# Linear attention's phi(k)^T v by two heads at a time, with the high and low halves of both operands side by side

## The chip, the core and the metric

The kernel runs on one core of one Trainium2 chip. The metric is device time in microseconds (us), lower is better. A run's time is that of the whole program. Engines are called by their names in the profile: PE is TensorE (matmul; PEld is its weight load), DVE is VectorE, ACT is ScalarE, POOL is GpSimd, SP is SyncE, whose queue issues most of the loads.

## What is computed

The reference mixes two branches over x (2048 tokens by 1024) with a gate per token. Branch A is linear attention with 32 heads of 32 columns; branch B is a GELU-gated MLP with 3584 hidden columns.

```python
g = _sigmoid((x * gate_w).sum(-1, keepdims=True))
a = _A_ref(x, A_wqkv, A_w_phi, A_wo)
b = _B_ref(x, B_w_gate, B_w_up, B_w_down)
return g * a + (1 - g) * b
```

The change lies in branch A, in the sums over tokens that every query needs:

```python
pk = jnp.einsum("bhsd,hdf->bhsf", k, w_phi)
phi_k = jnp.concatenate([_softmax(pk, axis=-1), _softmax(-pk, axis=-1)], axis=-1)
kv = jnp.einsum("bhsf,bhsd->bhfd", phi_k, v)
z  = jnp.einsum("bhsf->bhf", phi_k)
```

For each head, phi(k) has 64 columns (two softmaxes of 32), v has 32, and kv is a 64 by 32 matrix. z is the sum of phi(k) over the tokens.

## The kernel before

**Split numbers.** Nearly all products are made in the format fp32r. An fp32 operand is split in two fp32r parts: ScalarE copies it to the high part, VectorE subtracts that from the operand and gets the low part (`split`, lines 42 to 44). A product is then three passes: high by high, high by low, low by high (`PASSES`, line 24). Some small products stay in plain fp32: the folds and the sum z.

**Stages.** The first stage makes keys, values, phi(k)^T v and z. The second stage (line 721) makes the MLP's hidden layer and the queries in blocks by a scheme of seven products per 2 by 2 block, with the attention of the queries between them. The third (line 1100) makes the output. In all stages the instructions of PE and DVE run in the order in which the code is written, or put down by a small planner; the other engines' instructions of the first stage are put in order by the framework's scheduler.

**The first stage.** It runs in two halves of 16 heads (`hh`), and in each half over 16 chunks of 128 tokens. Ahead of the chunks, `fold` (lines 184 to 195) multiplies the key weights by w_phi as a block diagonal, so that keys come out as pk. Eight folded weight tiles serve one half. In each chunk:

- `keys_values` (lines 197 to 201): 8 blocks of the contraction by 3 passes by 2 outputs, keys and values, 48 matmuls of 512 columns. Both outputs lie in one PSUM tile of two banks (`two_banks`, line 58), of which there are two.
- `features` (lines 203 to 227), on DVE and ACT: the largest and the smallest pk of each head, the two differences (these four DVE passes read the keys' bank), the exponential (ACT), the split of the values into `vs`, the sums, the reciprocal, the scaling, the split of the features into `f`, and the addition to `zacc`, which collects z per partition.
- `accumulate` (lines 229 to 234): phi(k)^T v for the chunk two before the one whose keys were just made (`pending`). For each group of 4 heads one 128 by 256 block: the stationary operand is 128 columns of the values, the moving one two pieces of 128 features (the two softmaxes). 4 groups by 3 passes, 12 matmuls of 256 columns, into two banks that stay open over the half. Only the diagonal blocks of 32 are used.
- `meanwhile`: one block of x for the next chunks, or one step of the gate (line 171); two gate steps from chunk 11 of the second half on.
- In the second half `query_weights` (lines 275 to 285) folds the query weights, in chunks 3 to 10, with two groups of four plain fp32 products of 128 columns.

The last chunk of the first half is the turn: after each of its 8 contraction blocks comes the fold of one weight tile for the second half, and the features of chunk 14 run in steps between the folds.

**Ends of a half.** `finish_kv` (lines 236 to 240) turns the diagonal 32 by 64 blocks with 16 DVE transposes straight from PSUM into `kv_c`. `finish_z` (lines 242 to 254) multiplies a matrix of ones with `zacc` in plain fp32 and copies the results into `zb` by eight small ACT copies. Behind the second half (lines 374 to 390) TensorE makes the first projections of the MLP with what is left of the attention between them: g0, phi(k)^T v of chunk 14, g1, u0, z, phi(k)^T v of chunk 15, u1. POOL stores `kv_c` and `zb` to DRAM (lines 388 and 389), where the second stage reads them.

**The joint.** The second stage's buffers take the place of the first stage's. Lines 609 to 614 load four blocks of x (`raw`), the fourth into memory that the first stage's last tiles held; lines 466 to 469 are the sums of these blocks, lines 399 and 402 the high and low parts of sums and weights.

**Queues.** SP issues loads in program order; one that waits for memory holds up all behind it. POOL issues stores.

**PSUM.** Eight banks: two tiles of two banks (tag `pd`) for keys and values, four single banks (tag `pg`) of which phi(k)^T v holds two and folds, z and projections use the others.

Of the kernel before, what the change touches and what calls it, by code (L numbers as in the profile page):

```python
# [31 lines left out]
def tile_gated_mix(ctx: ExitStack, tc: tile.TileContext, x, xT, wkT, wqT, wv, w_phi, wo,  # L32
# [22 lines left out]
    def bank():  # L55
        return psum_g.tile([P, BLK], F32, tag="pg", name="pg", bufs=4)

    def two_banks():
        return psum_d.tile([P, 2, BLK], F32, tag="pd", name="pd", bufs=2)
# [77 lines left out]
    def fold_query(s, bp, k, pf):  # L137

        for j in range(4):
            nc.tensor.matmul(pf[:, j * P:(j + 1) * P], s[:, (4 * k + j) * P:(4 * k + j + 1) * P],  # L140
                             bp.rearrange("p a b -> p (a b)"), start=True, stop=True)
        nc.scalar.activation(s[:, k * BLK:(k + 1) * BLK], pf, AF.Copy)
# [3 lines left out]
    with tc.tile_pool(name="kw", bufs=1) as kw, tc.tile_pool(name="kp", bufs=1) as kp, \  # L146
            tc.manual_schedule(engines={PE, DVE}):
        ones = kp.tile([P, P], F32, name="ones")
        nc.vector.memset(ones, 1.0)
        phi_c = kp.tile([P, NG, 32], F32, name="phi_c")  # L150

        warm = two_banks()
        for _ in range(7):
            nc.tensor.matmul(warm[:, 0, :P], ones, ones, start=True, stop=True)
# [11 lines left out]
        kv_c = kp.tile([P, NG, 2, 32], F32, name="kv_c")  # L166
# [17 lines left out]
        def fold(hh, kc, bd, s=None):  # L184
# [3 lines left out]
            pf = bank()  # L188
# [8 lines left out]
        def keys_values(ps, w, b, t, kc):  # L197
            for i, (a, e) in enumerate(PASSES):
                for m in range(2):
                    nc.tensor.matmul(ps[:, m, :], xb[b, kc // 4][:, a, kc % 4, t * P:(t + 1) * P], w[:, e, m * 512:(m + 1) * 512],  # L200
                                     start=kc == 0 and i == 0, stop=kc == KC - 1 and i == 2)

        def features(ps, vs, f, zacc, first):

            pk = ps[:, 0, :].rearrange("p (h f) -> p h f", f=32)
# [8 lines left out]
            split(vs[:, 0, :], vs[:, 1, :], ps[:, 1, :])  # L214
# [14 lines left out]
        def accumulate(pkv, vs, f, first, last):  # L229
            for j in range(4):  # L230
                for i, (a, q) in enumerate(PASSES):
                    nc.tensor.matmul(pkv[j // 2][:, j % 2], vs[:, a, j * P:(j + 1) * P], f[:, q, :, j * P:(j + 1) * P],  # L232
                                     start=first and i == 0 and j % 2 == 0, stop=last and i == 2,
                                     skip_group_check=True)

        def finish_kv(hh, pkv):
            for j in range(4):
                for h in range(4):
                    q = slice(32 * h, 32 * h + 32)
                    nc.vector.transpose(kv_c[q, 4 * hh + j], pkv[j // 2][q, j % 2, :, 32 * h:32 * h + 32])  # L240

        def finish_z(hh, zacc):
            if hh:
                pz = two_banks()
                pz = [pz[:, s, :] for s in range(2)]
            else:
                pz = [bank() for s in range(2)]
            for s in range(2):
                nc.tensor.matmul(pz[s], ones, zacc[:, s].rearrange("p h f -> p (h f)"), start=True, stop=True)
            for s in range(2):  # L250
                z4 = pz[s].rearrange("p (g h f) -> p g h f", g=4, h=4)
# [23 lines left out]
        def query_weights(n):  # L275
            if staged:
                g, s, bp = staged.pop()
                for k in range(2):
                    fold_query(s, bp, k, bank())
                nc.gpsimd.dma_start(wq_fold[g], s)  # L280
            if 1 < n < 2 + NG:
                g = n - 2
# [6 lines left out]
        for hh in range(2):  # L289
            chunks = [(b, t) for b in ((0, 1, 2, 3) if hh == 0 else (2, 3, 0, 1)) for t in range(4)]  # L290
            ahead = []
            if hh == 0:

                ahead = [two_banks(), two_banks()]
# [28 lines left out]
            for n, (b, t) in enumerate(chunks):  # L323
# [3 lines left out]
                else:  # L327
                    ps = two_banks()
# [813 lines left out]
```

## Time and profile before

| | |
|---|---|
| median of 3 runs | 2396.36 us (2395.64 to 2396.86) |
| span of the execution profiled, the own time used below | 2395.1 us |
| PE busy | 2387.5 us, 10817 matmul records |
| first stage's key and value matmuls (line 200) | 1536 of 512 columns, from 8.6 to 429.0 us |
| phi(k)^T v (line 232) | 384 of 256 columns, from 47.9 to 451.5 us |
| DVE busy between 420 and 460 us | 37.7 of 40 us |
| first product of the second stage (line 721) | at 478.82 us |

The profile is one execution. A timeline row gives the start in us from the span's start, the length, the engine, the line of the kernel, the operation, the tile written and the tiles read, the shapes and the count; in brackets stand the idle time of the engine ahead of it and what ended it. A row of grouped instructions gives, behind the count, the busy time in us and the mean in ns of one instruction, then the idle time in front. A row of waits reads: who waited, for what, us in total, times, the longest. Matmuls overlap in their records, so the cost of one is read from the distance between starts. Plain fp32 matmuls appear as two records each.

### The profile page before, as it was taken

Reading aid. Unit: us, or ns where it says so; the run is one execution under the profiler, and the core shown is the slowest. Engines: PE = TensorE matmul, PEld = TensorE weight load, DVE = VectorE, ACT = ScalarE, POOL = GpSimd, SP = SyncE. Lnnn points to the kernel's source line nnn. Section 1 sums busy time; section 2 is a strip of 40 time slices with the busy share of each in tenths; the row PEclk is TensorE's granted clock in tenths of the full one; section 3 lists DMA queues with packets and bytes.
Section 4 is the critical chain, followed back from the end, with each engine's and each line's share of the span. In section 5 each row is a group of like instructions: output and inputs, shape, how many; then the busy total and the mean of one; then the engine's idle time right before and its main releaser. Section 6 shows DMA issues by size and latency. Waiting matters only on the chain.

```text
span 2395.1 us, 28363 instructions
## 1 busy us (share of the span) xinstructions
PE 2387.5 (100%) x10817; PEld 1986.0 (83%) x10817; DVE 1748.3 (73%) x2203; ACT 985.0 (41%) x1276; POOL 157.4 (7%) x294
## 2 busy tenths in 40 slices
PE   9999999999999999999999999999999999999999
PEld 8888888888888888888888888888888888888887
DVE  6877767857877877778777777777674778867873
ACT  4323232345454544455555555555533223323221
POOL 0000000011111112100000000000000000000000
PEclk9999999999999999999999999999999999999999
DMA  4112232544445456564334443443685767977874
GB/s 170 53 45 88 71 121 84 179 172 159 169 153 179 165 201 221 204 237 166 129 133 142 147 146 133 143 146 129 234 297 185 256 218 254 332 275 280 277 270 138
DMA packets 152569, 425.11 MB, mean 177 GB/s; under 512 B 21360, under 2 KB 21360, under 8 KB 152432
## 3 DMA queue, kind: packets, MB, share of 16 engines
q1 hardware_dynamic: 123840, 329.30, 40.7%
q0 software_dynamic: 27552, 93.87, 10.2%
q8 instruction: 84, 1.38, 0.2%
q14 instruction: 53, 0.43, 0.1%
q10 hardware_dynamic: 1040, 0.13, 0.0%
HBM read 328.34 MB, written 94.90 MB: 177 GB/s over the span
## 4 chain that ended last, share of the span: by engine, by line
PE 94%; DVE 3%; DMA 1%; ACT 1%; issue 1%; SPq 0%; ACTq 0%; DVEq 0%
PE po L1100 29%; PE a L721 20%; PE pd L200 14%; PE c L721 13%; PE b L721 7%; PE p L721 7%; PE misc L883 2%; PE pg L232 2%; PE pg L190 1%; PE pg L140 1%; DMA stage<-in_w_up 0%; DMA raw<-in_xT 0%; DMA stage<-in_w_gate 0%; DVE stage L171 0%; DMA early<-in_wkT 0%
## 5 line engine op out<-in xcount | busy, mean ns | idle before, releaser
L200 PE MATMUL pd<-wkv,x 128*128 128x512 f32 x1536 | 359.6, 392 | 0.0
L200 PEld LDWEIGHTS pd<-wkv,x 128*128 128x128 f32 x1536 | 286.3, 189 | 58.3 <-issue 0.5
L1100 PE MATMUL po<-tw,wgu 128*128 128x512 f32 x1344 | 309.8, 389 | 0.0
L1100 PEld LDWEIGHTS po<-tw,wgu 128*128 128x128 f32 x1344 | 252.3, 188 | 52.4
L399 ACT ACTIVATE wgu<-stage 128x1024 fp32r<-128x1024 f32 x147 | 155.1, 1055 | 244.7 <-DVE stage L990 160.4
L402 DVE TENSOR_TENSOR wgu<-stage,wgu 128x1024 fp32r<-128x1024 f32 x147 | 179.5, 1221 | 79.6 <-ACT wgu L399 78.6
L402 DVE TENSOR_TENSOR tyz<-stage,tyz 128x1024 fp32r<-128x1024 f32 x126 | 153.0, 1214 | 41.8 <-ACT tyz L399 41.8
L399 ACT ACTIVATE tyz<-stage 128x1024 fp32r<-128x1024 f32 x126 | 132.7, 1053 | 117.1 <-DVE stage L547 64.5
L721 PE MATMUL a<-s,tyz 128*128 128x512 f32 x744 | 179.4, 390 | 0.8 <-DVE tyz L402 0.4
L721 PE MATMUL b<-s,tyz 128*128 128x512 f32 x744 | 178.9, 389 | 0.1
L721 PE MATMUL a<-x,wgu 128*128 128x512 f32 x744 | 178.8, 389 | 0.0
L721 PE MATMUL c<-x,tyz 128*128 128x512 f32 x744 | 178.7, 389 | 0.0
L721 PE MATMUL p<-s,tyz 128*128 128x512 f32 x744 | 178.7, 389 | 0.0
L721 PE MATMUL a<-s,v 128*128 128x512 f32 x744 | 178.7, 389 | 0.0
L721 PE MATMUL c<-x,wgu 128*128 128x512 f32 x744 | 178.7, 389 | 0.0
L721 PEld LDWEIGHTS a<-s,tyz 128*128 128x128 f32 x744 | 139.4, 188 | 30.8 <-DVE tyz L402 1.3
L721 PEld LDWEIGHTS b<-s,tyz 128*128 128x128 f32 x744 | 139.6, 188 | 29.5 <-ACT b L756 0.5
L721 PEld LDWEIGHTS a<-x,wgu 128*128 128x128 f32 x744 | 139.6, 188 | 29.2 <-DVE h L696 0.2
L721 PEld LDWEIGHTS p<-s,tyz 128*128 128x128 f32 x744 | 139.7, 188 | 29.0
L721 PEld LDWEIGHTS c<-x,tyz 128*128 128x128 f32 x744 | 139.6, 188 | 29.0
L721 PEld LDWEIGHTS c<-x,wgu 128*128 128x128 f32 x744 | 139.6, 188 | 29.0
L721 PEld LDWEIGHTS a<-s,v 128*128 128x128 f32 x744 | 139.6, 188 | 29.0
(170 smaller groups left out, 3461.1 us busy)
## 6 DMA issues: line engine op xcount, KB each, us to landing
stage<-lm SPq DMA_DIRECT2D x98, 512.0 KB, 4.6
sr<-in_w_down SPq DMA_DIRECT2D x84, 512.0 KB, 5.0
sl<-lm SPq DMA_DIRECT2D x70, 512.0 KB, 4.8
lm<-h POOLq DMA_DIRECT2D x112, 256.0 KB, 2.5
stage<-in_w_gate SPq DMA_DIRECT2D x43, 512.0 KB, 3.7
stage<-in_w_up SPq DMA_DIRECT2D x43, 512.0 KB, 4.1
stage<-la SPq DMA_DIRECT2D x28, 512.0 KB, 4.8
tg<-stage POOLq DMA_DIRECT2D x26, 512.0 KB, 3.0
```

The costliest lines, as they stand in the source:

```text
L140: nc.tensor.matmul(pf[:, j * P:(j + 1) * P], s[:, (4 * k + j) * P:(4 * k + j + 1) * P], bp.rearrange("p a b -> p (a b)"), start=True, stop ...
L190: nc.tensor.matmul(pf[:, j * P:(j + 1) * P], s[:, j * P:(j + 1) * P], bd[:, j].rearrange("p a b -> p (a b)"), start=True, stop=True)
L200: nc.tensor.matmul(ps[:, m, :], xb[b, kc // 4][:, a, kc % 4, t * P:(t + 1) * P], w[:, e, m * 512:(m + 1) * 512], start=kc == 0 and i == 0, ...
L232: nc.tensor.matmul(pkv[j // 2][:, j % 2], vs[:, a, j * P:(j + 1) * P], f[:, q, :, j * P:(j + 1) * P], start=first and i == 0 and j % 2 == ...
L399: nc.scalar.activation(dst, src, AF.Copy)
L402: nc.vector.tensor_tensor(dst, src, dst_h.bitcast(F32), OP.subtract)
L721: nc.tensor.matmul(dst, w[:, h, 4 * part + kc, :], xq[:, e, kc, :], start=first and kc == 0 and i == 0, stop=kc == 3 and i == 2, skip_grou ...
L883: nc.tensor.matmul(po, kbs[:, a, s, :], pts[:, q, s, :], start=s == 0 and i == 0, stop=s == 1 and i == 2)
L1100: nc.tensor.matmul(ps[c], lefts[s][:, a, m, c * P:(c + 1) * P], made[k][:, e, m], start=d == 0 and m == 0 and n == 0, stop=d == n_duo - 1 ...
```

## The change

Five things are changed, all in the first stage.

1. phi(k)^T v: `vs` holds, for each pair of heads, 64 high columns and 64 low columns of the values side by side, which make one stationary operand of 128 columns. The moving operand is the high and low parts of both softmaxes' features of the same two heads, four pieces of 64 columns. One matmul per pair of heads makes all four combinations of parts, low by low too: 8 matmuls of 256 columns per chunk. The results lie in four open banks, which take the whole tag `pg`.
2. `finish_kv` adds the halves: ACT copies the columns of the high features, DVE adds those of the low features, ACT copies the rows of the low values beside those of the high ones, DVE adds them, then two wider transposes. The store is made by `finish_kv` itself, for each half, by two DMAs.
3. Keys and values lie in single banks (tag `pd`, now four of one bank). Outside the turn and the start, all 24 key matmuls come ahead of the 24 value matmuls. The folds of the turn, the query folds (one behind the keys, one behind the values, from chunk 4 on), the first z and the first projections use these four banks as well.
4. z: `zacc` is split into two parts in a weight buffer of the second stage or in one of `f`, and multiplied with ones in fp32r, two passes. At the end the order is g0, phi(k)^T v of chunk 14, the split of z, g1, u0, phi(k)^T v of chunk 15, u1, z.
5. ACT's copy of a folded query weight is marked urgent for the scheduler.

The core of the diff:

```diff
         def keys_values(ps, w, b, t, kc, parts=range(2)):
             for i, (a, e) in enumerate(PASSES):
-                for m in range(2):
-                    nc.tensor.matmul(ps[:, m, :], xb[b, kc // 4][:, a, kc % 4, t * P:(t + 1) * P], w[:, e, m * 512:(m + 1) * 512],
+                for m in parts:
+                    nc.tensor.matmul(ps[m], xb[b, kc // 4][:, a, kc % 4, t * P:(t + 1) * P], w[:, e, m * 512:(m + 1) * 512],
...
-            split(vs[:, 0, :], vs[:, 1, :], ps[:, 1, :])
+            split(vs[:, :, 0], vs[:, :, 1], ps[1].rearrange("p (a b) -> p a b", b=64))
...
         def accumulate(pkv, vs, f, first, last):
-            for j in range(4):
-                for i, (a, q) in enumerate(PASSES):
-                    nc.tensor.matmul(pkv[j // 2][:, j % 2], vs[:, a, j * P:(j + 1) * P], f[:, q, :, j * P:(j + 1) * P],
-                                     start=first and i == 0 and j % 2 == 0, stop=last and i == 2,
-                                     skip_group_check=True)
+            for d in range(8):
+                heads = slice(64 * d, 64 * d + 64)
+                nc.tensor.matmul(pkv[d // 2][:, d % 2], vs[:, d].rearrange("p a b -> p (a b)"), f[:, :, :, heads],
+                                 start=first and d % 2 == 0, stop=last, skip_group_check=True)
 
         def finish_kv(hh, pkv):
-            for j in range(4):
-                for h in range(4):
-                    q = slice(32 * h, 32 * h + 32)
-                    nc.vector.transpose(kv_c[q, 4 * hh + j], pkv[j // 2][q, j % 2, :, 32 * h:32 * h + 32])
+            t = kp.tile([P, 4, 2, 2, 64], F32, tag="e", name="kv_t", bufs=2)
+            for n, p in enumerate(pkv):
+                nc.scalar.activation(t[:, n], p[:, :, 0], AF.Copy)
+                nc.vector.tensor_tensor(t[:, n], p[:, :, 1], t[:, n], OP.add)
+            low_rows = kp.tile([P, 4, 2, 2, 64], F32, tag="e", name="kv_l", bufs=2)
+            nc.scalar.activation(low_rows[:64], t[64:], AF.Copy)
+            nc.vector.tensor_tensor(t[:64], t[:64], low_rows[:64], OP.add)
+            kv_c = kp.tile([P, 4, 2, 2, 32], F32, name="kv_c")
+            for h in range(2):
+                q = slice(32 * h, 32 * h + 32)
+                nc.vector.transpose(kv_c[q].rearrange("p a b c d -> p (a b c) d"),
+                                    t[q].rearrange("p a b c d -> p (a b c) d")[:, :, q])
+            for d in range(2):
+                nc.gpsimd.dma_start(kz[0][64 * d:64 * d + 64, 4 * hh:4 * hh + 4], kv_c[:64, :, d])
...
+        def z_parts(zacc, zs):
+            zs = zs.rearrange("p i (s a) b -> p i s (a b)", s=2)
+            split(zs[:, 0], zs[:, 1], zacc.rearrange("p s h f -> p s (h f)"))
+            return zs
+        def finish_z(hh, zs, parts=range(2)):
+            for s in parts:
+                pz = bank() if hh else turn_bank()
+                for i in range(2):
+                    nc.tensor.matmul(pz, ones_r, zs[:, i, s], start=i == 0, stop=i == 1)
...
-                    for kc in range(KC):
-                        keys_values(ps, wkv[kc], b, t, kc)
-                        if turn:
-                            fresh.append(fold(1, kc, bd))
+                        for kc in range(KC):
+                            keys_values(ps, wkv[kc], b, t, kc)
+                            fresh.append(fold(1, kc, bd, pf=turn_bank()))
                             next(steps, None)
+                    else:
+                        for m in range(2):
+                            for kc in range(KC):
+                                keys_values(ps, wkv[kc], b, t, kc, (m,))
+                            if hh:
+                                query_weights(n, m)
+                            if hh and n == 1:
+                                finish_z(0, zs, (m,))
...
-                        finish_z(0, zacc)
+                        zs = z_parts(zacc, new_weight())
...
-        first_g = {0: project(first_w[0], 0)}
+        first_g = {0: project(first_w[0], 0, turn_bank())}
         pending.pop(0)()
-        first_g[1] = project(first_w[0], 1)
-        pu = two_banks()
-        first_u = {0: project(first_w[1], 0, pu[:, 0, :])}
+        zs = z_parts(zacc, kp.tile([P, 2, KC, P], F32R, tag="f", name="zs", bufs=2))
+        first_g[1] = project(first_w[0], 1, turn_bank())
+        first_u = {0: project(first_w[1], 0, turn_bank())}
...
         second_w = weight(w_gate[1])
-        finish_z(1, zacc)
         pending.pop(0)()
-        nc.gpsimd.dma_start(kz[0], kv_c)
+        first_u[1] = project(first_w[1], 1, turn_bank())
+        finish_z(1, zs)
         nc.gpsimd.dma_start(kz[1], zb)
-        first_u[1] = project(first_w[1], 1, pu[:, 1, :])
```

More of the change, by code (lines that the diff above doesn't have):

```diff
@@ L165, in tile_gated_mix @@
         spare = [kp.tile([P, 1024], F32, tag="gw", name="early", bufs=1)] + spare
-        kv_c = kp.tile([P, NG, 2, 32], F32, name="kv_c")
         zb = kp.tile([P, NG, 2, 32], F32, name="zb")
@@ L273, in tile_gated_mix, with query_weights @@
         staged = []
-        def query_weights(n):
+        def query_weights(n, k):
             if staged:
[L277 to L282, printed above, removed]
+                g, s, bp = staged[0]
+                fold_query(s, bp, k, turn_bank())
+                if k:
+                    nc.gpsimd.dma_start(wq_fold[g], s)
+                    staged.pop()
+            if k and 2 < n < 3 + NG:
+                g = n - 3
                 bp = kp.tile([P, 4, 32], F32, name="bp", bufs=2)
@@ L292, in tile_gated_mix @@
             if hh == 0:
-                ahead = [two_banks(), two_banks()]
+                ahead = [[turn_bank(), turn_bank()] for _ in range(2)]
                 early = {}
@@ L366, in values @@
                     if n == 0:
-                        pkv += [psum_g.tile([P, 2, 2, P], F32, tag="pg", name="pg", bufs=4) for _ in range(2)]
+                        pkv += [bank((P, 2, 2, 2, 64)) for _ in range(4)]
                     accumulate(pkv, vs, f, n == 0, n == 15)
```

42 lines of the change are left out of this document (17 added, 25 removed).

## The prediction, made before the changed kernel ran

> **What bounds the kernel now.** I read the head of the page first, then the chain of work that ended last, then what TensorE waited for, then the timelines of the first stage.
>
> ```profile
> span 2395.1 us, 28363 instructions
> PE 2387.5 (100%) x10817; PEld 1986.0 (83%) x10817; DVE 1748.3 (73%) x2203; ACT 985.0 (41%) x1276; POOL 157.4 (7%) x294
> PE 94%; DVE 3%; DMA 1%; ACT 1%; issue 1%; SPq 0%; ACTq 0%; DVEq 0%
> ```
>
> TensorE is never free: 94% of the chain is its own work. So time comes off by taking matmuls away, as long as nothing else is late when TensorE comes earlier. The change touches only the first stage (keys, values and phi(k)^T v, up to about 460 us). What TensorE waits for at the joint behind that stage:
>
> ```profile
> PE a L721 <- DVE tyz L402: 0.4, 1, 0.4
> PE a L721 <- ACT c L754: 0.3, 1, 0.3
> ```
>
> Short, but not harmless: a wait of 0.4 us on VectorE says that VectorE's work there is just in time, with no slack to give.
>
> One chunk of 128 tokens, the turn between the halves (line 190 folds the second half's weights), and the sums z, on TensorE's timeline (start, length, form):
>
> ```profile
> 185.10 11.07 PE L200 MATMUL pd<-wkv,x 128*128 128x512 f32 x48
> 196.01 1.59 PE L232 MATMUL pg<-f,vs 128*128 128x256 f32 x12
> 197.44 1.55 PE L200 MATMUL pd<-wkv,x 128*128 128x512 f32 x6
> ...
> 229.37 1.88 PE L249 MATMUL pg<-zacc,ones 128*128 128x512 f32 x4
> 230.68 11.48 PE L200 MATMUL pd<-wkv,x 128*128 128x512 f32 x48
> 242.00 1.60 PE L232 MATMUL pg<-f,vs 128*128 128x256 f32 x12
> ```
> ```profile
> 448.45 1.88 PE L249 MATMUL pd<-zacc,ones 128*128 128x512 f32 x4
> 449.77 1.99 PE L232 MATMUL pg<-f,vs 128*128 128x256 f32 x12
> 451.59 5.63 PE L107 MATMUL pd<-x,wgu 128*128 128x512 f32 x24
> 457.06 21.92 PE L107 MATMUL pg<-x,wgu 128*128 128x512 f32 x96
> ```
>
> Starts are to be subtracted, since lengths overlap. 48 key and value matmuls: 196.01 - 185.10 = 10.91 us, 0.227 each. The 12 of phi(k)^T v: 197.44 - 196.01 = 1.43 us, 0.119 each.
>
> **The product phi(k)^T v.** Before, four groups by three passes make 12 matmuls of 256 moving columns per chunk. After, eight pairs of heads make 8, again of 256 columns: high and low values fill the stationary side, high and low features the moving side. Four fewer by 0.119 us, in 32 chunks: 4 x 0.119 x 32 = 15.2 us, all on the path. The Trainium skill ("TensorE: Matmul & The Clock Gate", section Back-to-back issue gap) gives a warm gap of N / 2.4 + 2.5 ns, 109 ns for 256 columns; by that estimate the sum would be 14.0 us. The trace's 0.119 differs from it and is used.
>
> **z.** The pair of fp32 products costs TensorE 230.68 - 229.37 = 1.31 us, and the group behind it starts slowly: 242.00 - 230.68 = 11.32 against 10.91. Together 1.72; at the end 1.32 and 1.82 - 1.43, 1.71. After, four split matmuls of 512 columns: 4 x 0.227 = 0.91. Saved twice: 1.6 us. TensorE's work shrinks by 15.2 + 1.6 = 16.8 us.
>
> **Keys, then values.** The same 48 matmuls, in runs into one bank. Line 107 runs 96 into single banks from 457.06; its group of 24 ahead takes 457.06 - 451.59 = 5.47, 0.228 each, so nothing here, within 0.9 us either way (0.03 per chunk). What it moves is VectorE: the four passes over the keys can start while the values are still being multiplied.
>
> ```profile
> 380.05 0.69 DVE L207 TENSOR_REDUCE mm<-pd 128x16 f32<-128x512 f32 x1 [2.26 <-PE pd L200]
> 384.21 0.69 DVE L44 TENSOR_TENSOR vs<-pd,vs 128x512 fp32r<-128x512 f32 x1 [0.53 <-ACT vs L43]
> 392.39 0.69 DVE L207 TENSOR_REDUCE mm<-pd 128x16 f32<-128x512 f32 x1
> 431.92 0.69 DVE L207 TENSOR_REDUCE mm<-pd 128x16 f32<-128x512 f32 x1
> ...
> 435.46 0.69 DVE L466 TENSOR_TENSOR raw<-raw 128x512 f32<-128x512 f32 x1
> ...
> 452.53 0.68 DVE L466 TENSOR_TENSOR raw<-raw 128x512 f32<-128x512 f32 x1
> 453.13 4.15 DVE L240 STREAM_TRANSPOSE kv_c<-pg 32x64 f32<-32x64 f32 x16
> 457.31 0.69 DVE L467 TENSOR_TENSOR raw<-raw 128x512 f32<-128x512 f32 x1
> 468.14 0.69 DVE L466 TENSOR_TENSOR raw<-raw 128x512 f32<-128x512 f32 x1 [2.82 <-DMA raw<-in_xT]
> ```
>
> In chunk 11 of the second half VectorE waits for TensorE until 380.05 and reads the values at 384.21, 4.2 us after they were ready. After, it reads them as soon as ScalarE has copied them:
>
> ```profile
> L43 ACT ACTIVATE vs<-pd 128x512 fp32r<-128x512 f32 x32 | 18.7, 584 | 0.0
> L44 DVE TENSOR_TENSOR f<-e,f 128x1024 fp32r<-128x1024 f32 x32 | 39.2, 1226 | 37.4 <-ACT f L43 37.4
> L43 ACT ACTIVATE f<-e 128x1024 fp32r<-128x1024 f32 x32 | 33.9, 1058 | 79.7 <-DVE e L220 79.6
> L254 ACT ACTIVATE zb<-pd 32x128 f32<-32x128 f32 x8 | 2.2, 270 | 2.7 <-PE pd L249 2.6
> L210 DVE TENSOR_TENSOR e<-pd,mm 128x512 f32<-128x512 f32 x32 | 21.8, 681 | 0.0
> L284 DVE TENSOR_TENSOR bp<-phi_c,mask 128x128 f32<-128x128 f32 x8 | 2.3, 284 | 0.0
> ```
>
> That is 0.7 us after their end (0.58 for the copy and a hand-over): 3.5 us won against TensorE. From chunk 11 on the chunks carry two gate steps, and VectorE's own period (392.39 - 380.05 = 12.34, with 0.1 idle) is longer than TensorE's new one (12.34 - 0.48 = 11.9). So from there VectorE runs back to back, and TensorE only fixes its starting point.
>
> **The joint.** The last step of the chunks is the turn of phi(k)^T v into its stored form, and its store frees the memory that the next stage loads into. The sync queue shows it (waits, then its issues):
>
> ```profile
> SPq L461 <- DMA kz<-zb: 19.3, 1, 19.3
> SPq L461 <- DMA kz<-kv_c: 4.6, 1, 4.6
> ```
> ```profile
> 435.57 0.34 SPq L51 DMA_DIRECT2D stage<-in_w_up  x1
> 460.00 0.88 SPq L461 DMA_DIRECT2D raw<-in_xT  x2
> 460.93 1.45 SPq L51 DMA_DIRECT2D stage<-in_w_gate  x2
> ```
> ```profile
> 457.58 0.55 POOL L388 DMA_DIRECT2D kz<-kv_c  x1 [4.13 <-DVE kv_c L240]
> ```
>
> The queue stands from 435.9 to 460.0, last for kv_c's store, with two weight loads behind the waiting one. The block of x lands at 468.14, and VectorE is then busy up to the product that waited 0.4 us. So this chain sets TensorE's next stage, and I follow its shift:
> - Chunk 11 ends earlier by 25 accumulations (16, then 9) x 0.476 + 0.8 for the first z = 12.7 us. VectorE wins 3.5 more: its last chunk (431.92) starts 16.2 us earlier.
> - Behind it the low part of z is new on VectorE (one pass of 1024: 1.2, ScalarE's 1.06 ahead of it filled by sums of x, as such waits are now).
> - Instead of 16 transposes (457.31 - 453.13 = 4.2) stand four adds of 256 (0.35 each, between the rows of 512 and 128; 1.4), a wait for ScalarE's copy of the low rows (1.06), an add of 1024 (1.2) and two transposes of 512 (0.7 each: 4.15 / 16 = 0.26 for 64 columns, and 448 more at the 1.03 ns that 681 - 284 over 384 columns gives; 1.4): 5.0, so 0.8 more. Behind the wait for ScalarE stand the sums of x; nobody but this store waits for its end. Two stores instead of one: 0.55 more on POOL.
> - Sum 1.2 + 0.8 + 0.55 = 2.6, so the load leaves 16.2 - 2.6 = 13.6 us earlier, at 446.4. z's own store, now behind the last accumulation and one projection, needs: the last accumulation's end, 451.59 - 15.2 - 0.8 - 1.7 = 433.9, the projection's 5.5, z's 0.9, ScalarE's eight copies at 2.2, and 2.7 to the store's end (457.31 to 460.0 for kv_c): 445.2, just ahead of it.
>
> TensorE would be 16.8 earlier, the chain 13.6: 3.2 us of TensorE's gain are waited away at the joint. Bounds: 4.4 if ScalarE's 1.06 ahead of the low part isn't filled, 0 if the sums of x that now precede 453.13 are put behind the store. I take 3.2, by the rows.
>
> **Banks.** phi(k)^T v holds all four banks of one pool, so folds go through the four single banks with keys and values. At the turn two dedicated banks become the two of chunk 14, whose values are read behind the first fold's parts:
>
> ```profile
> 201.01 0.68 DVE L44 TENSOR_TENSOR wkv<-pg,wkv 128x512 fp32r<-128x512 f32 x1
> 201.61 0.68 DVE L44 TENSOR_TENSOR vs<-pd,vs 128x512 fp32r<-128x512 f32 x1
> ```
> ```profile
> 201.10 1.05 PE L190 MATMUL pg<-bd,stage 128*128 128x128 f32 x8
> ...
> 203.37 1.05 PE L190 MATMUL pg<-bd,stage 128*128 128x128 f32 x8
> ```
>
> Folds are due every 203.37 - 201.10 = 2.3 us. Chunk 14's keys are read ahead of the turn, so the first fold has its bank; the second needs that of chunk 14's values, read last of the three VectorE passes behind the first fold (1.9 us with ScalarE's copy among them, and 1.4 us of matmuls to cover it): 0.5 (0 to 1.1). In the query chunks the keys' bank is back after VectorE's first 2.4 us (four passes of 0.6) and a fold's after one ScalarE copy, while at least 24 x 0.227 = 5.4 us of matmuls pass between two uses: nothing, and what a late bank would cost is rival 2. ScalarE's strided writes of the values and the copy marked urgent cost nothing, covered by ScalarE's idle time (41% busy); a copy slower by 0.1 us would, uncovered, cost 0.5 over the last five chunks, where VectorE waits for it. The copy of ones to fp32r at the start is one pass of 128 columns (0.28 at most) while TensorE runs its warm-up on the plain ones: nothing.
>
> Sum: 16.8 - 3.2 - 0.5 = 13.1 us, so 2395.1 - 13.1 = 2382.0 for the execution profiled. It stands 1.3 us under the median of 2396.36, which gives 2383.3.
>
> **Rivals.**
> 1. The joint moves with TensorE. If the scheduler puts the store of kv_c ahead of the sums of x, or z's store alone gates the load, all 16.8 us come out, with 0.9 for longer runs perhaps: 2396.4 - 16.8 - 0.9 = 2378.7 at best, 2379.5 as the value. For it: from 435.46 to 452.53 VectorE does eleven pieces of the next stage ahead of the store. Against: none of its rows from 431.92 to 457.31 has idle time in front, so it has no room to reorder into.
> 2. Banks in strict turn. At chunk 1 of the second half VectorE does the new turn of kv (5.0 us) ahead of the four key passes (2.4), and only then gives the bank back. If chunk 2's keys are handed that bank, TensorE stands 7.9 us: 2391.2. Against it: the z banks are free much earlier.
> 3. Slower: the moving operand. f is now read in four pieces of 64 columns, where it was two of 128. If TensorE pays for pieces, line 232's 256 remaining matmuls carry it. From 0.119 to 0.189 each the forecast gain and 4.8 us more are gone (17.9 / 256 = 0.070); at twice the pitch, 0.238, it is 30.5 more, 2413.8. Against it: two pieces already run at 0.119, near half of the 0.227 of 512 unbroken columns. The Trainium skill ("Advanced Engine Details and Errata", Memory Cachelines) says that a non-contiguous access pattern significantly slows matmuls, in its part on PSUM; the two-piece rows show nothing of it on the SBUF side.
> That the change leaves the work undone can't be: the four passes fewer are in the loop's count.
>
> **How the numbers follow.** A measurement here can tell about 0.2%, 4.8 us, from no change. Forecast 0.60, rival 1 0.18, rival 2 0.10, rival 3 0.05, unnamed stalls 0.07. Rival 2 lies at the edge, half faster and half the same; of the stalls 0.03 faster, 0.03 same, 0.01 slower. Faster 0.60 + 0.18 + 0.05 + 0.03 = 0.86, same 0.08, slower 0.06. The range goes from rival 1's best, 2378.5, to just past rival 2, 2392, and leaves out rival 3 and most stalls.
>
> **What would show it.** Line 232's successor: 256 matmuls, groups of 8 in 0.95 us. TensorE idle some 3 us at the joint, waiting on VectorE or ScalarE, with the last x load issued near 446. VectorE's key passes starting before the values end. Wrong: waits of keys_values for VectorE in the loop, a pitch above 0.13, or a joint with no new wait.

## The result and the profile after

| | before | after |
|---|---|---|
| median of 4 runs each | 2396.0 us (2395.05 to 2396.86) | 2383.35 us (2382.01 to 2385.03) |
| span of the execution profiled | 2395.1 | 2381.9 |

After takes 0.9949 of before's time, 95% interval 0.9935 to 0.9963: 12.65 us less by the medians, 13.2 by the two profiled spans. Forecast were 2383.3 and 13.1.

The head of the page after the change, to hold against that of before:

```profile
span 2381.9 us, 28130 instructions
PE 2370.9 (100%) x10689; PEld 1969.3 (83%) x10689; DVE 1748.3 (73%) x2188; ACT 994.1 (42%) x1288; POOL 158.8 (7%) x297
```

TensorE is busy for 16.6 us less (2387.5 - 2370.9); VectorE has as much to do as before. Less than 16.6 came out, so TensorE stands somewhere. What it waits for at the joint, from 425 to 500 us (total, times, longest):

```profile
PE c L698 <- DVE h L647: 2.3, 1, 2.3
PE a L739 <- DVE wgu L420: 0.6, 1, 0.6
PE a L739 <- ACT c L772: 0.4, 1, 0.4
```

That is 3.3 us, where before has only the 0.3 for ScalarE there: a new wait of 3.0. (The 0.4 us on VectorE's `tyz` that the prediction read as the joint's lies later in the second stage in both kernels, at 678.64 in before and 664.60 in after.) Later on, after has 0.7 us of waits in the third stage that are in neither before nor a second profile of the same kernel (e11, below): they belong to that execution.

TensorE's timeline after (start, length; starts are to be subtracted): the turn of the halves, the second half's first chunks with the products of z (line 264), and the end of the first stage.

```profile
188.85 1.11 PE L235 MATMUL pg<-f,vs 128*128 128x256 f32 x8
189.81 1.55 PE L202 MATMUL pd<-wkv,x 128*128 128x512 f32 x6
...
208.42 1.20 PE L235 MATMUL pg<-f,vs 128*128 128x256 f32 x8
...
226.79 0.62 PE L264 MATMUL pd<-wgu,ones_r 128*128 128x512 f32 x2
227.24 5.60 PE L202 MATMUL pd<-wkv,x 128*128 128x512 f32 x24
...
431.85 1.12 PE L235 MATMUL pg<-f,vs 128*128 128x256 f32 x8
432.81 5.63 PE L107 MATMUL pd<-x,wgu 128*128 128x512 f32 x24
438.27 1.07 PE L264 MATMUL pg<-zs,ones_r 128*128 128x512 f32 x4
439.18 22.20 PE L107 MATMUL pg<-x,wgu 128*128 128x512 f32 x96
```

Eight products take 0.96 us, 0.120 each (before: 0.119); z takes 0.45 twice in the first half and 0.91 at the end; the turn takes 208.42 - 189.81 = 18.61, where before it took 215.51 - 197.44 = 18.07 by the same rows. The list of TensorE's waits has no line for keys and values (202), so no chunk of the second half waits for a bank.

VectorE at the end of the first stage, in the order of time:

```profile
414.63 0.69 DVE L209 TENSOR_REDUCE mm<-pd 128x16 f32<-128x512 f32 x1
...
421.86 0.69 DVE L484 TENSOR_TENSOR raw<-raw 128x512 f32<-128x512 f32 x1 [1.87 <-DMA raw<-in_xT]
...
430.35 1.22 DVE L44 TENSOR_TENSOR zs<-zacc,zs 128x1024 fp32r<-128x1024 f32 x1
...
436.39 1.41 DVE L243 TENSOR_TENSOR kv_t<-pg,kv_t 128x256 f32<-128x256 f32 x4
...
439.04 1.21 DVE L246 TENSOR_TENSOR kv_t<-kv_t,kv_l 64x1024 f32<-64x1024 f32 x1
...
440.78 1.41 DVE L250 STREAM_TRANSPOSE kv_c<-kv_t 32x512 f32<-32x512 f32 x2
...
454.11 0.69 DVE L484 TENSOR_TENSOR raw<-raw 128x512 f32<-128x512 f32 x1 [2.91 <-DMA raw<-in_xT]
```

and the stores (POOL) and the load that stands for them (SP):

```profile
442.48 1.27 POOL L253 DMA_DIRECT2D kz<-kv_c  x2 [74.72 <-DVE kv_c L250]
443.74 0.56 POOL L408 DMA_DIRECT2D kz<-zb  x1
```
```profile
446.29 0.88 SPq L479 DMA_DIRECT2D raw<-in_xT  x2
```
```profile
467.26 0.50 PE L698 MATMUL c<-x 128*128 128x512 f32 x1 [2.32 <-DVE h L647]
```

The load leaves at 446.29; the forecast was 446.4. But the tail has grown. Call the **lag** the time from the end of the last accumulation (the start of what follows it on TensorE) to this load. Before it was 460.0 - 451.59 = 8.4 us, after it is 446.29 - 432.81 = 13.5: VectorE begins the turn 3.6 behind the accumulation (1.5 before), takes 5.8 to its end at 442.2 (4.2 before), and three stores leave behind one another.

The product of line 698, where TensorE waits, hangs on this load: in all twelve profiles that wait there it starts 20.75 to 21.04 us behind the load's issue (467.26 - 446.29 = 20.97 in after). In before it started 21.54 behind it and waited for nothing (481.54 - 460.00), so the chain there had an estimated 0.6 us of slack (21.54 less some 20.9).

**A start that differs.** The two profiles also differ where both kernels do the same. Stretches of the first microseconds of before; behind the busy times and counts of five engines stand the granted TensorE clock, the DMA share and GB/s:

```profile
7.00:8.00 1.00, 0.82 (x5) 0.82 (x6) 1.00 (x2) 0.22 (x1) 0.00 (x0) 0.73 0.93 318
8.00:9.00 1.00, 1.00 (x6) 1.00 (x6) 0.75 (x2) 0.41 (x1) 0.00 (x0) 0.50 1.03 389
9.00:10.00 1.00, 1.00 (x4) 0.81 (x3) 0.43 (x2) 0.93 (x2) 0.00 (x0) 0.50 1.06 412
10.00:11.00 1.00, 1.00 (x4) 0.75 (x4) 1.00 (x3) 0.71 (x2) 0.00 (x0) 0.56 1.05 406
11.00:12.00 1.00, 1.00 (x11) 0.95 (x9) 0.60 (x1) 0.00 (x0) 0.00 (x0) 1.00 1.05 397
```

and of after:

```profile
8.00:12.00 4.00, 4.00 (x26) 3.32 (x24) 3.55 (x6) 3.47 (x6) 0.00 (x0) 1.00 1.05 404
```

In before's profile the clock was at half for 0.54 + 1 + 1 + 0.88 = 3.4 us (0.54 and 0.88 being twice what 0.73 and 0.56 lack to one); in after's it wasn't. Of the 13 profiles of this study, before, e6 and e8 have the dip; the other ten, among them two of the same changed kernel, don't. It also shows in executions of one kernel: of the 39 executions of before that ran beside the experiments, 36 list a mean granted clock of 1.000 and have a median span of 2393.6, three list 0.999 (3.4 us at half in 2395 make 0.9993) and have 2394.4, 2394.5 and 2396.1. In e1, though, three executions with 0.999 are no longer than the other two. So the dip belongs to the execution and not to the kernel, and its price is less sure than its length. The Trainium skill ("TensorE: Matmul & The Clock Gate", Part 1) states a free-running window of 3.4 us whose position varies from run to run; the length agrees with these rows. In the profiles that have it, everything behind it is later: the accumulation that starts at 188.85 in after starts at 190.37 in e6, whose code up to there is the same; the last one ends 1.1 to 1.3 later (434.07 against 433.02 and 432.81), and 1.3 later in e8 than in e9 (433.70 against 432.37). So an estimated 1.2 us of the 13.2 between the two profiled spans, and of every shift read between them, are this and not the change.

### The profile page after: what moved, and what is told of

It is laid out like the page before. It is cut to its first block, busy times and chain, and to the rows that moved or that the text cites. A ratio compares the mean times of both kernels' runs of the same rounds, so it can differ in the third digit from the quotient of the medians.

```text
span 2381.9 us, 28130 instructions
## 1 busy us (share of the span) xinstructions
PE 2370.9 (100%) x10689; PEld 1969.3 (83%) x10689; DVE 1748.3 (73%) x2188; ACT 994.1 (42%) x1288; POOL 158.8 (7%) x297
## 4 chain that ended last, share of the span: by engine, by line
PE 75%; issue 3%; DMA 1%; DVE 1%; POOL 0%; ACT 0%; SPq 0%; POOLq 0%; DVEq 0%; ACTq 0%
PE po L1118 27%; PE a L739 20%; PE c L739 13%; PE b L739 7%; PE p L739 7%; PE misc L901 2%; DMA sr<-in_w_down 1%; POOL lm L135 0%; DVE sr L1040 0%; DVE tyz L420 0%; DMA lm<-h 0%; ACT tyz L417 0%; POOL la L135 0%; ACT L867 0%; DVE x L883 0%
```

## The experiments

Times are medians; "last acc." is the end of the last accumulation, "load" the issue of the x load, "joint" what TensorE waits from 425 to 500 us; "dip" marks the profiles with half the clock at the start (all in us, from the profile).

| run | time | ratio to before (95%) | last acc. | load | lag | joint |
|---|---|---|---|---|---|---|
| before (dip) | 2396.00 | | 451.59 | 460.00 | 8.4 | 0.3 |
| after | 2383.35 | 0.9949 (0.9935 to 0.9963) | 432.81 | 446.29 | 13.5 | 3.3 |
| e11, after again | 2382.69 | 0.9948 (0.9936 to 0.9961) | 433.02 | 446.43 | 13.4 | 3.2 |
| e1 | 2382.75 | 0.9946 (0.9934 to 0.9959) | 432.80 | 446.00 | 13.2 | 3.3 |
| e2 | 2380.87 | 0.9939 (0.9926 to 0.9951) | 432.88 | 444.29 | 11.4 | 1.5 |
| e3 | 2391.45 | 0.9984 (0.9975 to 0.9994) | 432.61 | 454.37 | 21.8 | 9.4 |
| e4 | 2399.33 | 1.0015 (1.0006 to 1.0024) | 448.19 | 462.23 | 14.0 | 3.6 |
| e5 | 2384.79 | 0.9956 (0.9943 to 0.9968) | 434.67 | 446.82 | 12.2 | 2.7 |
| e6 (dip) | 2383.86 | 0.9953 (0.9941 to 0.9966) | 434.07 | 448.96 | 14.9 | 3.8 |
| e7 | 2382.43 | 0.9947 (0.9933 to 0.9960) | 435.50 | 446.30 | 10.8 | 1.7 |
| e8 (dip) | 2380.61 | 0.9942 (0.9929 to 0.9954) | 433.70 | 445.46 | 11.8 | 1.8 |
| e9 | 2380.22 | 0.9936 (0.9923 to 0.9950) | 432.37 | 443.53 | 11.2 | 1.3 |
| e10 | 2379.25 | 0.9936 (0.9923 to 0.9948) | 432.33 | 442.94 | 10.6 | 0.8 |

Beside e1 to e4, run on one chip, before took 2395.41; beside e5 to e8 2395.43; beside e9 to e11 2395.10.

**e1: the block of x in other memory.** If the load stands because its buffer takes the place of z's or kv's, another place sets it free.

```diff
+        raw4 = fp.tile([P, 2, 2 * BLK], F32, tag="pts", name="raw", bufs=1)
         xs = [(xa if k < 2 else fp).tile(...) for k in range(4)]
...
-        raws.append(fp.tile([P, 2, 2 * BLK], F32, tag="pts", name="raw", bufs=1))
+        raws.append(raw4)
```

> Only the place of the fourth block of x is changed: its buffer is put ahead of two others, so that it falls on memory of the folded weights, which is free after the last key and value matmul. Theory (the joint is held by the stores of kv_c and z, which hold the sync queue): the queue no longer stands from 419 to 446 us, the block lands before 430, TensorE's waits at the joint (3.3 us in sum) fall to under 1 us, and the time falls by 2.5 us (1.5 to 3.3), to 2380.9. Rival (VectorE's amount of work at the joint is the bound, the load only fills a hole): the waits stay near 3 us and the time at 2383.3. Rival (time follows TensorE's work alone): 2383.3.

It left at 446.00, with the same waits behind it, and its queue still stood 25.9 us for kv_c's store and 0.9 for z's. The edit so did not set the load free, and the theory about the stores is not tested by it. Either a load into this pool waits for the last stores wherever in the pool it lies, or the new place overlaps what they read as well; no trace shows the addresses, and another pool wasn't tried.

**e2: the gate's passes behind the turn of kv.** In after, VectorE does two gate passes and sixteen small copies from 432 to 435, in front of the turn. The edit moves them behind the stores.

```diff
-        nc.scalar.activation(g_a, logit, AF.Sigmoid)
-        (g_b, g_n and the 16 copies to g_at)
         second_w = weight(w_gate[1])
         ...
         nc.gpsimd.dma_start(kz[1], zb)
+        nc.scalar.activation(g_a, logit, AF.Sigmoid)
+        (g_b, g_n and the 16 copies to g_at)
```

> The eighteen small VectorE passes of the gate (3.1 us) go from ahead of the turn of kv to behind it. Theory: kv_c's store leaves up to 3.1 us earlier; z's store, bound by TensorE's order (products until 439.2, copies until 441.7), then gates the load at about 444.3 instead of 446.3: 2.0 us less (1.0 to 2.5), 2381.3. Rival (VectorE's amount of work is the bound): the same work in another order, 2383.3.

VectorE's rows:

```profile
434.52 1.41 DVE L243 TENSOR_TENSOR kv_t<-pg,kv_t 128x256 f32<-128x256 f32 x4
...
438.80 1.41 DVE L250 STREAM_TRANSPOSE kv_c<-kv_t 32x512 f32<-32x512 f32 x2
...
440.40 3.25 DVE L408 COPY g_at<-g_a 32x16 f32<-32x16 f32 x16
```

The load leaves at 444.29, 2.0 us earlier, though TensorE's last accumulation ended at the same place (432.88). The waits at the joint shrink from 3.3 to 1.5, and the time from 2383.35 (2382.69 in e11) to 2380.87. So what VectorE does ahead of the turn sets when the load leaves, and the 2.0 us come back nearly one for one. (Of the 3.1 us that were moved the turn gained 1.9, 434.52 against 436.39: two more sums of x now stand ahead of it.)

**e3: the opposite dose.** The sixteen copies done twice, at their old place.

```diff
                 nc.vector.tensor_copy(g_at[...], g_a[...])
+                nc.vector.tensor_copy(g_at[...], g_a[...])
```

> The sixteen small copies of the gate are done twice: 3.0 us more on VectorE ahead of the turn of kv. Theory (VectorE up to kv_c's store sets the joint, with no slack): the store and the load behind it leave 2.9 us later, TensorE waits 6 us at the joint instead of 3.3, the time rises by 2.9 us (2.3 to 3.2) to 2386.2. Rival (time follows TensorE's work): VectorE has idle time at 446 and 451 us that takes it up, 2383.3.

The dose came out larger than meant: sums of x were scheduled between the copies, and the turn began at 444.53 instead of 436.39, 8.1 us later. The load left at 454.37, 8.1 later, and the time is 2391.45, 8.1 over after's 2383.35. TensorE stands in a second place too, since z's products need a bank that the adds give back:

```profile
445.10 2.05 PE L264 MATMUL pg<-zs,ones_r 128*128 128x512 f32 x4 [6.86 <-DVE kv_t L243]
...
475.37 0.50 PE L699 MATMUL c<-x 128*128 128x512 f32 x1 [2.10 <-DVE h L648]
```

z's four products then take twice as long as in after (2.05 against 1.07), for behind this idle time the granted clock was at half (columns as above, the clock third from the end):

```profile
441.00:450.00 9.00, 4.90 (x12) 3.91 (x13) 6.05 (x19) 3.20 (x9) 0.06 (x1) 0.50 0.00 0
```

With 0.64 in the microsecond ahead of this row and 0.74 in the one behind it, that is 0.72 + 9 + 0.52 = 10.2 us at half, from some 2 us after TensorE had stopped at 438.24. Neither the wait nor the slow clock is a price on top: the product of line 698 (here 699) starts at 475.37, 8.1 later than in after, like the load, and still waits 2.1 us.

So the expected size fails, and the law behind it holds in this kernel: a microsecond ahead of the turn is a microsecond of time.

**e4: the change without its saving.** Four of the eight products are issued twice (kv is then doubled for half of the pairs of heads), so that TensorE does 12 per chunk as before.

```diff
-            for d in range(8):
+            for d in (0, 1, 1, 2, 3, 3, 4, 5, 5, 6, 7, 7):
```

> Four of the eight products of phi(k)^T v per chunk are issued twice, so kv is doubled for every second pair of heads: TensorE has its 12 matmuls of 256 columns again (15.2 us more), all else as changed. Theory (of the 16.8 us taken from TensorE some 3 are waited away at the joint, because VectorE's chain follows TensorE only in part): the wait at the joint falls under 1 us, and the time rises by 11.5 us (10.5 to 12.5) to 2394.9, short of 15.2. Rival (every microsecond of TensorE counts in full): 15.2 more, 2398.6.

It is 16.0 us slower than after: the rival's figure, not the theory's. The theory was the prediction's account of the joint, that VectorE follows TensorE only in part, so that the wait vanishes where TensorE is slower. The wait is as long as ever, 3.6, and the lag 14.0:

```profile
446.75 1.59 PE L235 MATMUL pg<-f,vs 128*128 128x256 f32 x12
448.19 5.63 PE L107 MATMUL pd<-x,wgu 128*128 128x512 f32 x24
```
```profile
427.90 0.69 DVE L209 TENSOR_REDUCE mm<-pd 128x16 f32<-128x512 f32 x1
...
451.28 1.41 DVE L243 TENSOR_TENSOR kv_t<-pg,kv_t 128x256 f32<-128x256 f32 x4
...
455.67 1.41 DVE L250 STREAM_TRANSPOSE kv_c<-kv_t 32x512 f32<-32x512 f32 x2
```

With 15.2 us more room on TensorE, VectorE still begins the turn 3.1 us behind the accumulation. Its last chunk starts 13.3 us later than in after (427.90 against 414.63), so a part of the theory is there: VectorE did not follow the whole 15.2. But the room is filled. In e4 ten passes over blocks of x stand between that chunk's start and the turn, in after seven, at 0.6 to 0.7 us each, and z's store waits 1.1 us for ScalarE's copies where in after it follows the stores of kv. So the load leaves 15.9 later. The edit thus changed the order of the other engines' work too, and how long the wait would be in after's order isn't measured. As this kernel is put down, the joint moves with TensorE, and its 3 us come with the new tail. All of the change but the four products costs 3.9 us (2399.33 - 2395.41).

**e5: keys and values in turns again**, in the changed kernel.

```diff
-                        for m in range(2):
-                            for kc in range(KC):
-                                keys_values(ps, wkv[kc], b, t, kc, (m,))
+                        for kc in range(KC):
+                            keys_values(ps, wkv[kc], b, t, kc)
+                        for m in range(2):
```

> Of the changed kernel only the order of keys and values is undone: the matmuls of the two alternate again in every chunk, the two query folds follow behind both. TensorE's work is the same. Theory (keys first let VectorE start earlier, and its lead at chunk 11 is carried to the store of kv): VectorE reads the values 4.2 us behind their end instead of 1.9 to 2.7, the load of the last block of x leaves 1.5 to 3.5 us later, the time rises by 2.5 us (1.5 to 4.0) to 2385.9. Rival (the order of keys and values is worth nothing, time follows TensorE's work, as the run with twelve products suggested): 2383.3.

1.4 us slower than after by the medians, 2.1 than e11; the intervals overlap, so the time alone decides little. The waits on TensorE from 180 to 245 us, where after has none, show where it goes:

```profile
PE pd L202 <- ACT zb L268: 0.6, 1, 0.6
PE pd L192 <- DVE wkv L44: 0.3, 1, 0.3
PE pd L202 <- DVE wkv L44: 0.2, 1, 0.2
```

1.1 us are waits for banks at the turn and in the chunks behind it. VectorE's head start is there too. In e5 its last chunk starts at

```profile
418.24 0.69 DVE L209 TENSOR_REDUCE mm<-pd 128x16 f32<-128x512 f32 x1
```

3.6 later than after's 414.63, as forecast, but the load leaves only 0.5 later (446.82). Half of the lead goes into the 1.87 us that VectorE of after waits for a block of x at 421.86, where e5 waits for nothing. Most of the rest goes into the order: after does seven passes over blocks of x ahead of the turn, e5 five, and the turn starts only 0.4 later (436.83 against 436.39).

**e6: the last z in plain fp32**, as before.

```diff
+                if hh:
+                    nc.tensor.matmul(pz, ones, zs[:, s]..., start=True, stop=True)
+                else:
                     for i in range(2):
                         nc.tensor.matmul(pz, ones_r, zs[:, i, s], start=i == 0, stop=i == 1)
...
-        zs = z_parts(zacc, ...)
...
-        finish_z(1, zs)
+        finish_z(1, zacc)
```

> Only the second z, at the end of the stage, is made in plain fp32 again, from zacc itself; its place behind the last projection stays. TensorE has 0.8 us more work, VectorE 1.1 and ScalarE 1.0 less ahead of the store of kv. Theory (the store's lag behind the last accumulation sets the joint): the load leaves 1.1 us earlier and TensorE's 0.8 us lie in its wait, 1.1 less (0.3 to 1.6): 2382.2. Rival (time follows TensorE's work): 0.8 more, 2384.1.

0.5 over after and 1.2 over e11: nearer to the rival, and within the spread of the runs. The load did not leave earlier, as the theory had it. The lag is 1.4 longer, since z's store is now the last by far:

```profile
443.28 1.27 POOL L253 DMA_DIRECT2D kz<-kv_c  x2 [74.25 <-DVE kv_c L250]
446.51 0.56 POOL L410 DMA_DIRECT2D kz<-zb  x1 [1.97 <-ACT zb L271]
```

z is as much a part of this tail as kv. That splitting it pays behind the second half also is what the lag says; the time alone doesn't decide it.

**e7: before, with eight products**, the pass of the low values with the high features left out.

```diff
-                for i, (a, q) in enumerate(PASSES):
+                for i, (a, q) in ((0, (0, 0)), (2, (0, 1))):
```

> The kernel before, with the third of the three passes of phi(k)^T v left out (low values by high features): 8 matmuls of 256 columns per chunk in the old layout, all else as before. TensorE has 15.2 us less. Theory (without keys first VectorE follows TensorE only until chunk 11 of the second half, and then runs back to back at 12.25 us a chunk): the load of the last block of x leaves 12 us earlier, 12.2 us less than before (11.2 to 13.2), ratio 0.9949. Rival (time follows TensorE's work): 15.2 us less, ratio 0.9937.

13.0 us under before: on the theory's side, 2.2 short of the products' 15.2. VectorE's rows:

```profile
435.27 3.00 DVE L384 COPY g_at<-g_a 32x16 f32<-32x16 f32 x16
438.29 1.23 DVE L44 TENSOR_TENSOR wgu<-stage,wgu 128x1024 fp32r<-128x1024 f32 x1
439.43 4.14 DVE L240 STREAM_TRANSPOSE kv_c<-pg 32x64 f32<-32x64 f32 x16
```

The accumulation ends at 435.50, and the gate's copies and a weight's low part, which before did ahead of that moment, now stand between it and the turn: the lag grows from 8.4 to 10.8, and TensorE waits 1.7 us at the joint where before waits 0.3. The rest of the 2.2 is lost at the turn of the halves, which takes 18.92 (189.62 to 208.54) against 18.07; two of its folds wait for the loads of their weights. So in the old kernel 1.4 of the saving is lost at the joint, for the most part behind VectorE, and some 0.8 at the turn.

**e8: e2, and the values of chunk 14 read ahead of the first fold.**

```diff
                         fresh = []
+                        next(steps, None)
                         for kc in range(KC):
```

> The gate's small passes behind the turn of kv, as in the run that had them there, and at the turn between the halves chunk 14's values are split ahead of the first fold instead of behind it, so that their bank is free for the second fold. Theory (the turn lost 0.5 us for want of a bank: 18.6 us where it took 18.1): the turn takes 18.1 us, 0.5 less than the run with the late gate alone (0.3 to 0.6): 2380.4. Rival (the half microsecond is the price of folds into these banks, not a wait): no change, 2380.9.

The times don't part the two expectations. The turn does, on TensorE:

```profile
191.26 1.55 PE L202 MATMUL pd<-wkv,x 128*128 128x512 f32 x6
...
209.32 1.20 PE L235 MATMUL pg<-f,vs 128*128 128x256 f32 x8
```

18.06 us, before's 18.07, and e9 and e10, which keep this edit, have 18.06 and 18.08. The changed kernel's turn without it takes 18.37 to 18.67 in after, e11, e1 to e4 and e6. So the 0.3 to 0.6 that it loses there is the bank of chunk 14's values, as named.

**e9 and e10: the rest of the tail.** e9 is e8 with the second of the two stores of kv issued by SP; e10 is e9 with z's products in the middle of the up projection.

```diff
-                nc.gpsimd.dma_start(kz[0][...], kv_c[:64, :, d])
+                (nc.sync if hh and d else nc.gpsimd).dma_start(kz[0][...], kv_c[:64, :, d])
```
```diff
-        first_u[1] = project(first_w[1], 1, turn_bank())
-        finish_z(1, zs)
+        first_u[1] = project(first_w[1], 1, turn_bank(), lambda: finish_z(1, zs))
```

> Edit: the gate passes behind the key-value turn, the values of chunk 14 ahead of the first fold (as in the run before this one), and in the second half the second store of keys and values issued by SyncE, not by GpSimd behind the first. Theory, that the joint's length is a chain of VectorE's turn and of three stores in one queue of 0.56 to 0.64 us each, the last of which lets the load of x leave: one place of the queue goes, so the load leaves 0.5 us earlier than in the run without this edit (445.46, or 444.29 where the first twelve microseconds ran at full granted clock), and the time is 2380.1 (2379.5 to 2380.7). Rival, that z's copies, which end at 441.22 in the run with late gates, set the end and not the queue: no change, 2380.6.

> Edit: as in the run with the second queue, and z's four products put into the middle of the up projection (2.7 us earlier) instead of behind it. Theory: z's store then leaves before those of keys and values, the load of x leaves some 0.6 us earlier than with the second queue alone, TensorE's wait of 1.1 us for the sums of x at the joint shrinks by as much, and the time is 2379.6 (2379.0 to 2380.2). Rival, that ScalarE takes z's copies ahead of the copy of the low rows, which holds VectorE's turn back by up to 2.2 us: the load leaves up to 1.5 us later, and the time is 2381.5 to 2382.

In e9 z's store waits for ScalarE's copies, so the place in the queue is worth little (lag 11.2 against 11.4 in e2, which has no dip either): mostly the rival's answer, though the time, 2380.22, lies between the two.

```profile
441.01 0.54 POOL L403 DMA_DIRECT2D kz<-zb  x1 [0.69 <-ACT zb L268]
```

The load leaves 0.8 us earlier than in e2, and 0.5 of that is the accumulation, which ends earlier by what the turn of the halves saves. In e10 z is ready in time:

```profile
439.58 0.55 POOL L404 DMA_DIRECT2D kz<-zb  x1 [72.30 <-ACT zb L270]
440.11 0.64 POOL L255 DMA_DIRECT2D kz<-kv_c  x1
```
```profile
PE a L741 <- ACT c L774: 0.4, 1, 0.4
PE c L700 <- DVE h L649: 0.4, 1, 0.4
```

The load leaves at 442.94, 0.6 earlier than in e9, and 0.8 us of waits are left at the joint. That is the theory's answer on the load. 2379.25 us (2379.01 to 2381.09) is the lowest median of the study, 3.4 under e11 on the same chip; its runs overlap with those of e9 (2379.34 to 2380.5), so the step from e9 to e10 rests on the rows and not on the time.

**e11: after, unedited.**

> The changed kernel itself, unedited, once more. In the profiles so far the granted clock from 8 to 12 us was either 0.61 to 0.64 (before, and two of the edited kernels) or 1.00 (after, and the other edited kernels), whatever the kernel, and where it was low everything behind it came 1.3 to 1.5 us later. If that is a matter of the execution, this kernel can show either; if it shows the low one, its last accumulation ends near 434.1 instead of 432.8 and its span is near 2383.2 instead of 2381.9. The time of several rounds is 2383.3 (2382.3 to 2384.3) if the four rounds that the first result rests on gave it rightly.

Full clock at the start, the same lag and joint as in the first profile. Pooled with the first four runs, after takes 2382.0 to 2385.0.

## Why the prediction came out right, step by step

- **Four products fewer, 15.2 us.** Right: the pitch of eight products with a moving operand in four pieces is 0.120. Rival 3, a price for pieces, is out. The 109 ns that the Trainium skill ("TensorE: Matmul & The Clock Gate", section Back-to-back issue gap) gives for 256 columns is lower than the pitch here in either form. e4 and e7 show what these products are worth: 16.0 in the new kernel, 13.0 in the old.
- **z, 1.6 us.** Right on TensorE (0.90 and 0.91 us).
- **The turn, 0.5 us.** Right in size (0.54 in after, 0.3 to 0.6 over all profiles) and, by e8, in cause.
- **Banks in strict turn (rival 2).** Out: behind the turn of the halves no key or value product waits. (Its 7.9 us is also 0.5 more than the two terms it names, 5.0 and 2.4.)
- **The joint, 3.2 us.** Right in size, though one of the two waits that it was argued from lay elsewhere: TensorE waits 3.0 more there, and the load left 0.1 from the time forecast. But that hit is made of misses. The chain's shift of 13.7 holds some 1.2 that is the clock's dip in before's profile, so the change itself moved the load by 12.5, not 13.6. The 16.2 us at the head of the chain were right on that footing (431.92 - 414.63 = 17.3, less 1.2). Three terms behind it were not. From the last chunk to the turn VectorE takes 0.55 more than before (21.76 and 21.21), where 1.2 more was forecast: the wait of 1.87 us for a block of x was missed, and so was that seven passes of the next stage stand there, not eleven. The turn takes 5.8 where 5.0 was forecast, for two sums of x and a low part lie in it. And from the turn's end to the load it takes 4.1 us, 1.4 more than before, where 0.55 was forecast, since z's store now comes third in the queue. The forecast also gave the chain no slack, where before had some 0.6. TensorE itself reaches the second stage 17.6 earlier (461.21 against 478.82), 16.4 without the dip: the forecast's 16.8 less the 0.5 of the turn. 16.4 less 12.5 and 0.6 is 3.3, near the 3.0 measured.
- **The reason given for the joint** holds only in part. The step was: "from there VectorE runs back to back, and TensorE only fixes its starting point", so TensorE's saving can't all be followed. (The 0.1 us of idle time that it reads counts only the gap ahead of the next chunk; within the 12.34 us VectorE also waits 0.53 and 1.13 for ScalarE.) e4 gives the products back, and VectorE's last chunk moves by 13.3 and not by 15.2, as the step says. But the wait at the joint stays, since the passes ahead of the turn and z's store move too, which the forecast took as fixed. What stands, shown by e2, e3 and e10, is that the tail behind the last accumulation is too long: gate passes ahead of the turn (2.0 us), and z behind a projection and at the end of a queue of three stores. That the copy by ScalarE in the turn costs time is read from the rows and was not tried. In the old kernel the joint takes back 1.4 of the saving too, for the most part in VectorE's queue (e7).
- **Rival 1** (the joint moves with TensorE) had the load's movement right for the changed kernel (15.9 for 15.2 in e4) and the time wrong, for it left out that the new tail is longer.

What is left open: 16.8 less 3.0 and 0.5 is 13.3, and the medians show 12.4 to 12.65, which is within their spread.

## What to carry to other kernels

Work taken off the bound engine is given back at the next joint unless the tail behind it is as short as before: time the tail from the end of the bound work to the transfer that waits, and put the other engines' unrelated passes behind it. Before two profiles are subtracted from each other, compare a stretch in which both kernels do the same; here 1.2 us of 13 lay there. A total that comes out right shows no cause: the experiment that took the saving away left in place a wait that the reason for it said would go.

## What the hardware showed that was not expected

- The granted clock fell to 0.50 for 3.4 us between 7 and 11 us in 3 of 13 profiles, behind an idle time of TensorE of 1.4 us (1.41 in before); other executions with the same idle time (1.42 in after) kept 1.00. In e3 it was at 0.50 for 10.2 us, three times as long, around an idle time of 6.9 us, and fell some 2 us into that time.
- A moving operand in four pieces of 64 columns costs as much as one in two of 128, within 0.001 us: 0.120 against 0.119 us for 256 columns.
